# Spacer tiles that shift where the float32r operands of a fused retention and two-layer MoE kernel begin in SBUF

## The chip, the cores and the metric

The kernel runs on one core of a Trainium2 chip. The metric is device time of one execution in microseconds (us); lower is better. Engines: PE is TensorE (PEld its weight loads), DVE VectorE, ACT ScalarE, POOL GpSimd, SP SyncE, which issues most transfers.

## The reference

```python
def _attn_ref(q, k, v):            # (4, 8, 768, 64) each
    gamma = 1.0 - 2.0 ** (-5.0 - np.arange(H))
    for t in range(S):
        state = gamma * state + einsum('bhd,bhe->bhde', k[:, :, t], v[:, :, t])
        y[:, :, t] = scale * einsum('bhd,bhde->bhe', q[:, :, t], state)
...
def _moe_ref(x, w_gate, w_val, w_out, rms_g):     # 3072 tokens, 512 -> 1536 -> 512
    xn = x / sqrt(mean(x * x) + 1e-06) * rms_g
    g = xn @ w_gate
    return silu(g) * (xn @ w_val) @ w_out
...
def _moe2_ref(x, w_in, w_out, g_ln):              # 512 -> 1024 -> 512
    h = x @ w_in
    solu = h * softmax(h)
    return (layernorm(solu) * g_ln) @ w_out
```

The weights arrive as 64-bit floating-point numbers, which the kernel turns into float32 itself.

## The kernel before

The 3,072 tokens go through in six blocks (`n`, 0 to 5) of 512. Of each block the kernel computes the retention (`att_*`, in chunks of 128 tokens), the root-mean-square norm, the gated layer (`bc_block`) and the second layer (`de_block`). Attention of block n+1 is cut into pieces that are called from slots between the matmuls of block n, so that TensorE is never without work; the order on the engines follows the order of the calls and of a scheduler.

The large matmuls run in float32r on operands that were split into a high and a low part (`split`, lines 86 and 87), and each product is three matmuls: `mm3` (lines 561 to 563).

```python
nc.tensor.matmul(ps, lhsT=lh, rhs=rh, start=start, stop=False)
nc.tensor.matmul(ps, lhsT=lh, rhs=rl, start=False, stop=False)
nc.tensor.matmul(ps, lhsT=ll, rhs=rh, start=False, stop=stop)
```

Here `lhsT` is loaded into the array as weights (128 columns of 4 bytes, 512 bytes in each partition) and `rhs` is streamed (512 columns, 2,048 bytes). Four places call it:

- `gv`: gate and value, 12 groups `g` of 128 hidden columns in each block. It loads w4 tiles (in the trace `w`), or CV for odd groups of block 0, and streams xnh and xnl. 24 matmuls a group into the banks GB and VB (the first group of all in halves of 256 columns).
- `cmm`: output of the gated layer. It loads wo tiles or, for odd groups of block 0, CV, and streams r2 tiles (`r`). 12 matmuls a group into X0 to X3.
- `d_mm`: first product of the second layer. It loads x2 tiles (`x`) and streams w2ih and w2il. 24 matmuls for each of 4 token tiles of a block.
- `e_mm`: second product. It loads r2 tiles and streams w2oh and w2ol. 24 matmuls for each token tile (the last of all in halves).

In block 0 the weights are loaded as 64-bit words (`load64`), turned into float32 (`conv`), split, used, and stored to `scr` in HBM; blocks 1 to 5 load the split form from there (`w_load`).

SBUF tiles come from two pools, `cp` (fixed tiles) and `wp` (rings of buffers). They are laid out one behind another in the order in which the program first asks for their tags, each rounded up to 32 bytes, so every tile has a fixed byte address in its partition. Slices that TensorE loads or streams begin at whole multiples of 512 bytes inside their tile, so a tile's address modulo 512 is that of all its slices. Before the change these are:

| tiles | address modulo 512 |
|---|---|
| w2ih (with QK), w2il (with KV), xT, xnh, xnl, U, ssq, w2oh | 128 |
| w2ol, which is also CV; mtab, qtab | 224 |
| ident | 384 |
| the rings: x2, r2, f4, st, w4, wo, rq, rk, rv, kd, qd, kst, qhl, A | 448 |

Of the kernel before, what the change touches and what calls it, by code (L numbers as in the profile page):

```python
# [9 lines left out]
F32 = mybir.dt.float32  # L10
F32R = mybir.dt.float32r
# [7 lines left out]
P = 128  # L19
# [21 lines left out]
def retention_moe_kernel(ctx: ExitStack, tc: tile.TileContext, qk0, q2, kt, kv, wpk, w2i, w2o,  # L41
                         rg, gl, sel, mtab, qtab, ktab, utab, out):
    nc = tc.nc
    cp = ctx.enter_context(tc.tile_pool(name="cp", bufs=1))
# [11 lines left out]
    EB = [GV[0], XB[1], XB[2], XB[3]]  # L56


    QK = cp.tile([P, NCB, 2, 4, P], F32, tag="w2ih", name="QK")
    KV = cp.tile([P, NCB, 2, 512], F32, tag="w2il", name="KV")  # L60
    w2 = {}
# [10 lines left out]
    def wt(tag, shape, dt, bufs):  # L72
        cnt[0] += 1
        return wp.tile(shape, dt, tag=tag, name=f"{tag}_{cnt[0]}", bufs=bufs)
# [10 lines left out]
    def split(hi, lo, src, lo_eng=None):  # L85
        nc.scalar.copy(hi, src)  # L86
        (lo_eng or nc.vector).tensor_tensor(out=lo, in0=src, in1=hi.bitcast(F32), op=ALU.subtract)  # L87
# [119 lines left out]
    def att_yu(gc, u, Y):  # L207
# [4 lines left out]
        if u:  # L212
            sq = f4()[:, 0, :].rearrange("p (a i) -> p a i", a=4)
            nc.scalar.activation(sq, xT[:, :, cs], AF.Square)
            nc.vector.tensor_reduce(out=ssq[:, cs], in_=sq.rearrange("p a i -> p i a"), axis=AX.X, op=ALU.add)

    rinv = cp.tile([P, NCB], F32, tag="rinv", name="rinv")

    def rms_1(bank):
# [86 lines left out]
    def first_load(c):  # L306
        nc.sync.dma_start(QK[:, c], qk0[c])
        nc.sync.dma_start(KV[:, c], kv[c].rearrange("u p x -> p u x"))

    def first_scores(c, banks, halves=(0, 1)):  # L310

        for hh in halves:
            r = slice(64 * hh, 64 * hh + 64)
            for p in range(4):
                nc.tensor.matmul(banks[hh][:, p * P:p * P + P], lhsT=QK[r, c, 1, p, :], rhs=QK[r, c, 0, p, :],
                                 start=True, stop=True)
# [19 lines left out]
    def first_qd(c):  # L336
        qd = wt("r2", [P, 4, P], F32, 8)
        nc.gpsimd.tensor_tensor(out=qd, in0=QK[:, c, 0], in1=qtab_t, op=ALU.mult)
        return qd
# [85 lines left out]
    NG = NB * NM  # L425

    scr = [[dp.tile([P, 2, 512], F32, tag=f"scr{m}_{p}", name=f"scr{m}_{p}") for p in range(3)] for m in range(NM)]
    CV = cp.tile([P, 4, 2, 512], F32R, tag="w2ol", name="CV")

    wide = {}  # L430

    def load64(key):
# [53 lines left out]
    def wtile(part):  # L486
        return wt("w4" if part < 2 else "wo", [P, 2, 512], F32R, 4 if part < 2 else 2)
# [15 lines left out]
    def w_split(g, part):  # L503
# [3 lines left out]
        t = done64.pop((g, part))  # L507
        w = wtile(part) if g % 2 == 0 else CV[:, part if part < 2 else 2 + g // 2 % 2]
        split(w[:, 0, :], w[:, 1, :], t, nc.gpsimd if 0 < g and (part + g) % 2 else nc.vector)
# [251 lines left out]
    def warm(n, bank, rhs):  # L761
        for _ in range(n):
            nc.tensor.matmul(bank[:, 0:P], lhsT=ones, rhs=rhs, start=True, stop=True)

    warm(WARM, GV[1], ones)
    nc.sync.dma_start(QK[:, 0], qk0[0])
    nc.sync.dma_start(mtab_t, mtab)
# [13 lines left out]
    make_identity(nc, ident)  # L781
    mhalf = cp.tile([P, 16], F32, tag="mhalf", name="mhalf")
    nc.gpsimd.memset(mhalf, -0.5)
    nc.gpsimd.memset(U0, 0.0)
    for t in U:
        nc.gpsimd.memset(t, 0.0)
# [178 lines left out]
```

## Time and profile before

| | |
|---|---|
| time, three runs | 1050.81, 1052.34 (median), 1052.58 us |
| profiled execution: span from the first to the last instruction | 1049.7 us |
| PE busy | 1028.7 us, 98% |
| PEld busy | 818.8 us, 78% |
| DVE, ACT, POOL busy | 52%, 39%, 31% |
| DMA | 181.10 MB, mean 173 GB/s |

Of the profiled execution nothing is known beside its span; the runs' median is 2.6 us above it. Matmuls overlap, and their ends are modelled, so a matmul's own duration (about 400 ns for 512 columns) is longer than the distance between the starts of two of them. The rate of TensorE is read from starts in the timeline.

### The profile page before, as it was taken

The numbers are of one execution on the slowest core, as the hardware profiler recorded it, in microseconds if no ns is written. First come the engines' busy times: TensorE is split into PE (matmuls) and PEld (weight loads), VectorE is DVE, ScalarE is ACT, GpSimd is POOL, SyncE is SP. The second block draws the span as 40 slices with busy tenths as digits, with TensorE's granted clock in tenths as the row PEclk, the third lists the DMA queues.
The fourth block names the chain that finished last, engine by engine and source line by source line (L and its number), as shares of the span: only waits on it lengthen the run. The fifth ranks groups of instructions, "written<-read, shape, count | busy, mean of one in ns | idle before, by whom it ended". The sixth has DMA issues, their size and how long they took to land.

```text
span 1049.7 us, 14176 instructions
## 1 busy us (share of the span) xinstructions
PE 1028.7 (98%) x5174; PEld 818.8 (78%) x5174; DVE 542.9 (52%) x1014; ACT 412.2 (39%) x785; POOL 329.4 (31%) x414
## 2 busy tenths in 40 slices
PE   9999999999999999999999999999999999999998
PEld 7877776777878887777777777778777777888887
DVE  5887676886376633344682343482435466111162
ACT  3666655564344432223352232343322325111243
POOL 6886773774134311111250011141211014000031
PEclk9899999999999999999999999999999999999999
DMA  9699996886612015566303566501655510455301
GB/s 345 215 341 382 340 364 260 300 311 211 202 50 71 11 61 190 181 213 206 113 21 118 201 203 221 190 21 30 216 196 200 176 56 21 141 195 185 101 1 41
DMA packets 60485, 181.10 MB, mean 173 GB/s; under 512 B 7168, under 2 KB 7552, under 8 KB 60416
## 3 DMA queue, kind: packets, MB, share of 16 engines
q1 hardware_dynamic: 51632, 155.03, 43.5%
q10 hardware_dynamic: 8784, 25.17, 6.1%
q8 instruction: 41, 0.67, 0.3%
q14 instruction: 28, 0.23, 0.1%
HBM read 153.96 MB, written 26.21 MB: 172 GB/s over the span
## 4 chain that ended last, share of the span: by engine, by line
PE 84%; DVE 7%; DMA 3%; issue 2%; POOL 2%; ACT 1%; SPq 0%; ACTq 0%; POOLq 0%; DVEq 0%
PE X L562 11%; PE X L563 11%; PE X L561 11%; PE GB L561 7%; PE GB L563 7%; PE GB L562 7%; PE VB L561 7%; PE VB L563 7%; PE VB L562 7%; PE YB L158 1%; PE SB L138 1%; DVE st L466 1%; DVE r L87 1%; PE YB L155 1%; DVE st L479 1%
## 5 line engine op out<-in xcount | busy, mean ns | idle before, releaser
L578 DVE TENSOR_TENSOR f<-VB,f 128x512 f32<-128x512 f32 x72 | 49.6, 689 | 171.5 <-PE VB L563 156.1
L128 POOL TENSOR_TENSOR qd<-rq,qtab_t 64x256 f32<-64x256 f32 x68 | 56.5, 831 | 228.8 <-PE YB L155 148.4
L561 PE MATMUL GB<-xnh,w 128*128 128x512 f32 (+1 forms) x268 | 107.3, 400 | 0.2 <-ACT w L86 0.2
L561 PE MATMUL VB<-xnh,w 128*128 128x512 f32 (+1 forms) x268 | 107.1, 400 | 0.0
L562 PE MATMUL GB<-xnl,w 128*128 128x512 f32 (+1 forms) x268 | 106.4, 397 | 0.0
L563 PE MATMUL GB<-xnh,w 128*128 128x512 f32 (+1 forms) x268 | 106.0, 396 | 0.3 <-DVE w L87 0.3
L562 PE MATMUL X<-r,wo 128*128 128x512 f32 x264 | 104.5, 396 | 0.9 <-DVE r L87 0.9
L563 PE MATMUL VB<-xnh,w 128*128 128x512 f32 (+1 forms) x268 | 105.3, 393 | 0.0
L562 PE MATMUL VB<-xnl,w 128*128 128x512 f32 (+1 forms) x268 | 105.2, 393 | 0.0
L563 PE MATMUL X<-r,wo 128*128 128x512 f32 x264 | 103.7, 393 | 0.0
L561 PE MATMUL X<-r,wo 128*128 128x512 f32 x264 | 98.3, 397 | 0.5 <-ACT r L86 0.5
L606 ACT ACTIVATE f<-GB 128x512 f32<-128x512 f32 x72 | 42.8, 595 | 137.4 <-PE GB L563 136.7
L86 ACT CAST r<-f 128x512 fp32r<-128x512 f32 x72 | 44.6, 619 | 115.6 <-DVE f L578 115.2
L467 POOL TENSOR_TENSOR st<-st,x 128x512 int32<-128x512 int32 x52 | 69.9, 1345 | 41.5 <-ACT x L464 12.0
L87 DVE TENSOR_TENSOR r<-f,r 128x512 fp32r<-128x512 f32 x72 | 60.9, 845 | 30.0 <-ACT r L86 29.6
L144 DVE TENSOR_TENSOR A<-SB,s 128x256 f32<-128x256 f32 x64 | 27.0, 422 | 94.3 <-ACT s L142 94.0
L678 POOL TENSOR_TENSOR sm<-sm 128x1 f32<-128x1 f32 x24 | 5.3, 223 | 205.2 <-DVE sm L656 173.4
L142 ACT COPY s<-SB 128x256 f32<-128x256 f32 x64 | 24.0, 374 | 101.7 <-PE SB L138 101.7
L561 PEld LDWEIGHTS GB<-xnh,w 128*128 128x128 f32 x268 | 51.1, 191 | 12.5 <-issue 0.9
L563 PEld LDWEIGHTS GB<-xnh,w 128*128 128x128 f32 x268 | 51.0, 190 | 11.7 <-DVE w L87 0.8
L561 PEld LDWEIGHTS VB<-xnh,w 128*128 128x128 f32 x268 | 50.6, 189 | 12.1 <-issue 1.2
L563 PEld LDWEIGHTS VB<-xnh,w 128*128 128x128 f32 x268 | 50.5, 188 | 12.2 <-POOL w L87 0.4
(241 smaller groups left out, 2359.9 us busy)
## 6 DMA issues: line engine op xcount, KB each, us to landing
w<-scr SPq DMA_DIRECT2D x120, 512.0 KB, 3.3
wo<-scr SPq DMA_DIRECT2D x60, 512.0 KB, 3.3
x<-in_wpk SPq DMA_DIRECT2D x36, 512.0 KB, 6.2
rq<-in_q SPq DMA_DIRECT2D x40, 256.0 KB, 3.3
rv<-in_kv SPq DMA_DIRECT2D x40, 256.0 KB, 3.6
scr<-CV ACTq DMA_DIRECT2D x18, 512.0 KB, 6.3
scr<-w ACTq DMA_DIRECT2D x12, 512.0 KB, 6.4
out<-f ACTq DMA_DIRECT2D x23, 256.0 KB, 2.0
```

Source lines behind the costliest of these rows:

```text
L86: nc.scalar.copy(hi, src)
L87: (lo_eng or nc.vector).tensor_tensor(out=lo, in0=src, in1=hi.bitcast(F32), op=ALU.subtract)
L128: nc.gpsimd.tensor_tensor(out=qd[r], in0=tq4[r, :, hh, :], in1=qtab_t[r, 2 * u:2 * u + 2, :], op=ALU.mult)
L138: nc.tensor.matmul(SB[:, hh * 256:hh * 256 + 256], lhsT=kst[:, hl + hh, :], rhs=qhl[:, hl + hh].rearrange("p s i -> p (s i)"), start=True, ...
L142: nc.scalar.copy(s2, s4[:, :, 1, :])
L144: nc.vector.tensor_tensor(out=A, in0=s4[:, :, 0, :], in1=s2, op=ALU.add)
L467: nc.gpsimd.tensor_tensor(out=ti, in0=ti, in1=lo, op=ALU.add)
L561: nc.tensor.matmul(ps, lhsT=lh, rhs=rh, start=start, stop=False)
L562: nc.tensor.matmul(ps, lhsT=lh, rhs=rl, start=False, stop=False)
L563: nc.tensor.matmul(ps, lhsT=ll, rhs=rh, start=False, stop=stop)
L578: nc.vector.tensor_tensor(out=a, in0=GV[1], in1=silu[:, 0, :], op=ALU.mult)
L606: nc.scalar.activation(s[:, 0, :], GV[0], AF.Silu)
```

## The change

Two spacer tiles, of 320 and 192 bytes in each partition, are allocated and never written or read. The tile CV, with the tag that w2ol takes over, is asked for earlier, before the small tiles rinv and rsum. Nothing else is touched, and the instructions of all five engines stand in the same order as before, with the same waits.

```diff
@@ -56,6 +56,10 @@
     EB = [GV[0], XB[1], XB[2], XB[3]]
 
 
+    def spacer(n, name):
+        cp.tile([P, n // 4], F32, tag=name, name=name)
+
+    spacer(320, "sp0")
     QK = cp.tile([P, NCB, 2, 4, P], F32, tag="w2ih", name="QK")
     KV = cp.tile([P, NCB, 2, 512], F32, tag="w2il", name="KV")
     w2 = {}
@@ -214,6 +218,7 @@
             nc.scalar.activation(sq, xT[:, :, cs], AF.Square)
             nc.vector.tensor_reduce(out=ssq[:, cs], in_=sq.rearrange("p a i -> p i a"), axis=AX.X, op=ALU.add)
 
+    CV = cp.tile([P, 4, 2, 512], F32R, tag="w2ol", name="CV")
     rinv = cp.tile([P, NCB], F32, tag="rinv", name="rinv")
 
     def rms_1(bank):
@@ -425,8 +430,6 @@
     NG = NB * NM
 
     scr = [[dp.tile([P, 2, 512], F32, tag=f"scr{m}_{p}", name=f"scr{m}_{p}") for p in range(3)] for m in range(NM)]
-    CV = cp.tile([P, 4, 2, 512], F32R, tag="w2ol", name="CV")
-
     wide = {}
 
     def load64(key):
@@ -781,6 +784,7 @@
     make_identity(nc, ident)
     mhalf = cp.tile([P, 16], F32, tag="mhalf", name="mhalf")
     nc.gpsimd.memset(mhalf, -0.5)
+    spacer(192, "sp1")
     nc.gpsimd.memset(U0, 0.0)
     for t in U:
         nc.gpsimd.memset(t, 0.0)
```

The addresses modulo 512 after it:

| tiles | before | after |
|---|---|---|
| w2ih (with QK), w2il (with KV), xT, xnh, xnl, U, ssq, w2oh | 128 | 448 |
| w2ol, CV | 224 | 448 |
| the rings (x2, r2, f4, w4, wo, qd, ...) | 448 | 448 |
| mtab, qtab | 224 | 32 |
| ident | 384 | 192 |

The rings lie 512 bytes higher than before, and the tiles of the first row 320 bytes higher.

## Rows read from the trace of the kernel before

**Rows 1.** The page, busy time of the engines, and TensorE's granted clock in 40 slices.
```profile
PE 1028.7 (98%) x5174; PEld 818.8 (78%) x5174; DVE 542.9 (52%) x1014; ACT 412.2 (39%) x785; POOL 329.4 (31%) x414
...
PEclk9899999999999999999999999999999999999999
```

**Rows 2.** The page, the chain that ended last, shares by engine.
```profile
PE 84%; DVE 7%; DMA 3%; issue 2%; POOL 2%; ACT 1%; SPq 0%; ACTq 0%; POOLq 0%; DVEq 0%
```

**Rows 3.** TensorE's waits, whole span: total us, times, longest us.
```profile
PE GB L563 <- DVE r L87: 2.8, 2, 1.8
PE X L562 <- DVE r L87: 2.8, 3, 1.9
```

**Rows 4.** Groups of matmuls by shape: count | busy us, mean ns | idle before.
```profile
L561 PE MATMUL VB<-xnh,w 128*128 128x512 f32 x260 | 104.8, 403 | 0.0
...
L561 PE MATMUL X<-r,wo 128*128 128x512 f32 x264 | 98.3, 397 | 0.5 <-ACT r L86 0.5
...
L669 PE MATMUL X<-ident,f 128*128 128x128 f32 x120 | 17.9, 273 | 1.5 <-POOL f L658 1.5
```

**Rows 5.** Timeline of TensorE, block 5: start us, us, instruction; 24 of `gv`, 12 of `cmm`.
```profile
919.96 0.39 PE L561 MATMUL GB<-xnh,w 128*128 128x512 f32 x1
...
925.56 0.39 PE L561 MATMUL X<-r,wo 128*128 128x512 f32 x1
...
926.25 0.40 PE L561 MATMUL X<-r,wo 128*128 128x512 f32 x1
926.49 0.39 PE L562 MATMUL X<-r,wo 128*128 128x512 f32 x1
926.72 0.39 PE L563 MATMUL X<-r,wo 128*128 128x512 f32 x1
...
928.08 0.39 PE L563 MATMUL X<-r,wo 128*128 128x512 f32 x1
928.30 0.39 PE L561 MATMUL GB<-xnh,w 128*128 128x512 f32 x1
```

**Rows 6.** Timeline of the weight loads beside the first of them.
```profile
920.20 0.19 PEld L563 LDWEIGHTS GB<-xnh,w 128*128 128x128 f32 x1
```

**Rows 7.** Timeline, block 0: `cmm` with CV, 12 intervals.
```profile
64.66 0.40 PE L561 MATMUL X<-r,CV 128*128 128x512 f32 x1
...
67.45 0.39 PE L561 MATMUL GB<-xnh,CV 128*128 128x512 f32 x1
```

**Rows 8.** Timeline, block 0: two `cmm` with wo (11 intervals from 76.14; 9 from 95.54).
```profile
75.81 0.50 PE L561 MATMUL X<-r,wo 128*128 128x512 f32 x1
76.14 0.39 PE L562 MATMUL X<-r,wo 128*128 128x512 f32 x1
...
78.68 0.39 PE L561 MATMUL GB<-xnh,w 128*128 128x512 f32 x1
...
95.54 0.39 PE L561 MATMUL X<-r,wo 128*128 128x512 f32 x1
...
97.58 0.39 PE L561 MATMUL X<-r,wo 128*128 128x512 f32 x1
```

**Rows 9.** Timeline: `e_mm`, 37 intervals, and `d_mm`, 24 intervals.
```profile
324.50 0.40 PE L562 MATMUL X<-w2ol,r 128*128 128x512 f32 x1
...
333.06 0.39 PE L563 MATMUL X<-w2oh,r 128*128 128x512 f32 x1
...
873.63 0.40 PE L561 MATMUL VB<-w2ih,x 128*128 128x512 f32 x1
...
879.23 0.39 PE L561 MATMUL GB<-xnh,w 128*128 128x512 f32 x1
```

**Rows 10.** Busy us of PE, PEld, DVE, ACT, POOL in three stretches, granted clock, DMA share, GB/s.
```profile
35.00:168.00 133.00, 129.85 (x681) 101.78 (x680) 104.07 (x149) 86.26 (x149) 100.11 (x91) 0.97 0.92 339
168.00:350.00 182.00, 176.52 (x868) 140.56 (x867) 117.74 (x209) 86.95 (x169) 77.39 (x85) 1.00 0.53 181
350.00:520.00 170.00, 170.00 (x859) 134.83 (x858) 75.41 (x153) 54.58 (x109) 33.50 (x57) 1.00 0.44 147
```

## The prediction

> **What bounds the kernel now.** I read the totals first: TensorE's matmuls are in flight for 98% of the span, at a granted clock of 9 or more tenths in every slice but one [rows 1], so nearly all of the run is at the higher of its two levels, 2.4 GHz. A busy TensorE isn't proof of a limit, because matmuls overlap, so I went to the chain of work that ended last: 84% of it is TensorE, 7% VectorE, 3% DMA [rows 2]. Then TensorE's own waits: the longest totals are 2.8 us [rows 3]. Nothing that another engine does holds TensorE up for long; what sets the time is how fast TensorE gets from one matmul to the next. Most of these are float32r matmuls of 512 columns. By the loops there are 3,696: 71 full groups in `gv` of 24 (1,704), 72 calls of `cmm` of 12 (864), 24 of `d_mm` of 24 (576), 23 full ones of `e_mm` of 24 (552). The groups of instructions agree: 264 for the first matmul of `cmm` with wo, a third of 792 [rows 4].
>
> The duration in those rows, about 0.40 us, is no price: matmuls overlap. The price is the distance from one start to the next, so I took the timeline. In the last attention-free stretch a block of 24 `gv` matmuls runs from 919.96 to 925.56 us: 5.60/24 = 233.3 ns each. The 12 of `cmm` that follow run to 928.30: 2.74/12 = 228.3 ns, and the six intervals from 926.72 to 928.08 take 1.36/6 = 226.7 [rows 5]. So the same instruction with the same shape has two paces. What differs is where operands lie. While a matmul streams, the weights of the next one are loaded: the load that starts at 920.20 us beside the second matmul is that of the third, and is in flight for 0.19 us [rows 6]. In `cmm` the streamed tile (r2) and the loaded one (wo) both begin at 448 modulo 512; in `gv` the streamed xnh and xnl begin at 128, the loaded w4 at 448.
>
> Two more places bear that out. The `cmm` whose weights lie in CV (224) streams the same r2 tiles in the same order, and takes 2.79/12 = 232.5 ns, with no quick end [rows 7]; so it isn't that `cmm` streams the same two tiles over and over. And an aligned `cmm` in the same busy stage runs at 226.7 ns (2.04/9) from its first matmul [rows 8]. `d_mm` (128 against 448) stands at 5.60/24 = 233.3; `e_mm`, which streams 128 and 224 by turns against 448, at 8.56/37 = 231.4 [rows 9].
>
> **The change part by part.** No instruction is added, removed or moved: the order on all five engines is the same, waits included. The spacers are never written, so they cost no time. Only addresses change, and of these the ones that matter put all float32r tiles at 448, the place that `cmm` with wo has today. DMA writes into the ring buffers keep their place modulo 512.
>
> *The intervals.* 3,696 matmuls stand in 170 unbroken runs in TensorE's order (attention, transposes or sums stand between them). I leave out each run's last interval and its first, which is a start (75.81 to 76.14 is 0.33 us) [rows 8]: 3,696 - 340 = 3,356. Of these 792/3,696 are aligned now, 719. The rest is unaligned: `gv` and `d_mm` 2,280/3,696, 2,070; `e_mm` 501; `cmm` with CV 65. Settled aligned pace: 226.7 ns. So: 2,070 x (233.3 - 226.7) = 13.7 us; 501 x (231.4 - 226.7) = 2.4; 65 x (232.5 - 226.7) = 0.4; and the 719, whose groups are now cut off after 12, 719 x (228.3 - 226.7) = 1.2. Together 17.6 us.
>
> *The price of a start.* An aligned run doesn't always settle at once. After an attention piece one group needed 2.54 us for 11 intervals, 46 ns over 11 x 226.7 [rows 8]; the one behind `gv` needed 1.16 us for its first five, 27 ns over [rows 5]; the one at 95.54 nothing [rows 8]. Bounds 0 and 46 ns a run; I take 20, nearer to the middle case, since some start settled: 170 x 20 ns = 3.4 us. Bounds 0 and 7.8 us. Left: 14.2 us.
>
> *What is late next.* A quicker TensorE asks earlier for what others deliver. From 350 to 520 us VectorE is busy 75 of 170 us and GpSimd 34, and TensorE without a gap: room enough. But in the first block, 35 to 168 us, the DMA engines are busy 92% at 339 GB/s, with VectorE at 104 of 133 us [rows 10]. Its 432 matmuls carry 432/3,696 of the gain, 1.7 us. If the transfers set the pace there, all of it is lost; if not, none; TensorE's waits on converted weights are short but the transfers have little slack, so I take half, 0.8 us. Between 168 and 350 VectorE has 118 of 182 us, and I charge nothing. Left: 13.4 us.
>
> *The other tiles.* `ident` goes from 384 to 192 while the transposed f4 stays at 448; U goes from 128 to 448, where qd is. No row shows either pair at its new place. The two paces of the 512-column form differ by 7 ns; with that either way on the 192 transposes, 120 of which have a row [rows 4], the bound is 1.3 us up or down, and I take zero. The 256-column pieces of `gv` and `e_mm`, 96 matmuls, could give 0.6 us; left out of the sum, kept in the range. Tables that VectorE and GpSimd read (mtab, qtab, utab, ssq) move too: hidden behind TensorE's work, at those engines' idle shares.
>
> Sum: 13.4 us off the profiled execution's 1049.7 us gives a span of 1036.3. The median of the runs is 2.6 us above that span, and I carry this over: 1038.9, say 1039.0 us.
>
> **A rule against it.** The rows show two paces that go with the operands' places [rows 5, 7]. The Trainium skill, page "TensorE: Matmul & The Clock Gate", section "Step-by-step: what each phase is for", says that the array has two independent read ports, and that loading the next tile's weights takes no bandwidth from the running matmul. By that rule the places can't matter and the sum would be 0. The trace doesn't agree: 232.5 and 226.7 ns in one form of instruction with the same streamed tiles.
>
> **The rivals.** *Nothing happens* (1052.3 us): the place of the tiles isn't what parts the two paces, but something that goes with them, such as the engine activity around a `cmm`, or CV being written nearby. For it: `e_mm` at 231.4 lies between, with no aligned pair, so the place modulo 512 alone doesn't make the pace. Against it: the two `cmm` of [rows 7, 8], 31 us apart, the same code, one with CV and one with wo. Chance 0.09. The Trainium skill's rule above (page "TensorE: Matmul & The Clock Gate") gives this case too.
>
> *Slower.* With both at 448, weight load and stream start at the same byte modulo 512, and in long runs of one kind (`gv`: 24) they meet each other again and again, where `cmm`'s runs of 12 end early. The longest intervals among the aligned rows are 0.24 us (926.25 to 926.49) [rows 5]. Locked there, `gv` and `d_mm` lose 6.7 ns, `e_mm` 8.6, `cmm` 11.7: `cmm` with CV 7.5: 13.9 + 4.3 + 8.4 + 0.5 = 27 us, 1079. It decides from a mean above 231.9 ns, which is the weighted mean of today's four paces. Against it: after the sixth matmul the aligned group stays at 226.7. Chance 0.05.
>
> *Most is given back* (1044 to 1048): every run pays 46 ns and the first two blocks, some 30% of the matmuls, keep nothing because DMA and VectorE set their pace. 17.6 - 7.8 = 9.8; less 30%, 6.9; 1045.4. Chance 0.08.
>
> **How the numbers follow.** My forecast has 0.78; its own range is 1034 (no start cost, nothing lost: 1052.3 - 17.6 = 1034.7, and 0.6 for the 256-column pieces) to 1044.3 (46 ns a run and the first block lost: 17.6 - 7.8 - 1.7 = 8.1). To hold eight in ten the range goes on to 1046, into the third rival. About 0.2%, 2.1 us, is what a measurement of this kernel can tell from no change. Faster: 0.78 + 0.08 = 0.86; same 0.09; slower 0.05.
>
> **What would show it.** In the timeline of 900 to 1000 us a `gv` block of 24 should take 5.44 us instead of 5.60, a block of 36 with its `cmm` 8.16 instead of 8.34. `d_mm` should fall from 233.3 to about 227, `cmm` with CV from 232.5, and aligned `cmm` with wo should show its quick end from the first matmul where `gv` stands ahead. If `gv` stays at 233, the places don't matter and I am wrong at the root; if it falls, but the time doesn't, look at the first block's DMA and at what starts cost. The clock should stay as it is, and the order of instructions too. I would also be wrong if the settled pace turned out to hang on the distance in steps larger than 512 bytes, which the spacers leave as they are.

## The result, and the profile after

The changed kernel takes 1041.62 us (median of 4 runs, 1040.31 to 1042.41), the kernel before 1052.46 in the runs taken with it: ratio 0.9901, 95% interval 0.9871 to 0.993. That is 10.8 us of gain; 13.4 were forecast, and 1041.62 lies inside the range of 1034 to 1046. The four runs of the kernel before include one of 1066.30 us; the other three have a median of 1052.34. The profiled execution has a span of 1038.5 us against 1049.7.

The page of the changed kernel, beside [rows 1, 2]:

```profile
PE 1014.7 (98%) x5174; PEld 817.8 (79%) x5174; DVE 542.5 (52%) x1014; ACT 412.5 (40%) x785; POOL 329.5 (32%) x414
...
PEclk9999998999999999999999999999999999999999
...
PE 80%; DVE 8%; issue 4%; POOL 4%; ACT 2%; DMA 1%; SPq 0%; ACTq 0%; POOLq 0%; DVEq 0%
```

Busy shares, clock and counts are nearly as they were, and the reader learns little from them: TensorE is still "98% busy", and it has 80% of the chain where it had 84%. What changed is seen in starts. The timeline of TensorE in block 5, beside [rows 5] (start us, us, instruction; `mm3` is now at lines 564 to 566), and `d_mm`, beside [rows 9]:

```profile
865.86 0.39 PE L564 MATMUL VB<-w2ih,x 128*128 128x512 f32 x1
...
871.30 0.39 PE L564 MATMUL GB<-xnh,w 128*128 128x512 f32 x1
...
919.40 0.39 PE L564 MATMUL GB<-xnh,w 128*128 128x512 f32 x1
...
922.12 0.39 PE L564 MATMUL VB<-xnh,w 128*128 128x512 f32 x1
...
924.84 0.39 PE L564 MATMUL X<-r,wo 128*128 128x512 f32 x1
...
927.56 0.39 PE L564 MATMUL GB<-xnh,w 128*128 128x512 f32 x1
```

24 `gv` matmuls go from 919.40 to 924.84: 5.44 us, 226.7 ns each, where [rows 5] had 5.60. The 12 of `cmm` behind them take 2.72 us, and the 36 together 8.16. `d_mm` has 5.44/24 = 226.7 as well. The matmul's own duration is still 0.39: only the distance between starts shows the change.

Block 0 on the same view, beside [rows 7, 8]: a `cmm` with CV, and the `cmm` with wo that starts after an attention piece.

```profile
64.86 0.39 PE L564 MATMUL X<-r,CV 128*128 128x512 f32 x1
...
67.58 0.39 PE L564 MATMUL GB<-xnh,CV 128*128 128x512 f32 x1
...
76.15 0.39 PE L565 MATMUL X<-r,wo 128*128 128x512 f32 x1
...
78.67 0.39 PE L564 MATMUL GB<-xnh,w 128*128 128x512 f32 x1
```

With CV: 2.72/12 = 226.7, where it was 232.5. With wo: 2.52 us for 11 intervals, 27 ns over the settled pace (before: 46).

**Where the time came from.** The 5,174 matmuls of the two traces pair off one to one, in the same order. I split the distances between successive 512-column matmuls at 300 ns. The short ones, some 3,370, fell from a mean of 232.2 to 228.1 ns: 13.7 us less. The long ones, which hold waits and stretches at half pace, grew by 3.8 us, all of it in the first 195 us (nine distances passed from short to long, and of those only what exceeds the short mean is counted here). Everything else fell by 1.2 us. Sum: 13.7 - 3.8 + 1.2 = 11.1 us. So TensorE's own gain is what was forecast, and the shortfall is in waits.

One place carries most of that. TensorE in block 0 after the change, where `cmm` waits for r2 (in brackets: idle time, and who ended it):

```profile
162.90 1.21 PE L564 MATMUL X<-r,CV 128*128 128x512 f32 x4 [1.94 <-ACT r L90]
...
165.97 0.79 PE L565 MATMUL X<-r,CV 128*128 128x512 f32 x1 [1.85 <-DVE r L91]
166.56 0.63 PE L566 MATMUL X<-r,CV 128*128 128x512 f32 x1
166.98 0.63 PE L565 MATMUL X<-r,CV 128*128 128x512 f32 x1
...
169.12 0.63 PE L566 MATMUL X<-r,CV 128*128 128x512 f32 x1
```

and the same two waits in the kernel before:

```profile
161.73 1.19 PE L561 MATMUL X<-r,CV 128*128 128x512 f32 x4 [0.48 <-ACT r L86]
...
164.82 0.50 PE L562 MATMUL X<-r,CV 128*128 128x512 f32 x1 [1.90 <-DVE r L87]
```

The first wait is 1.5 us longer after the change, although TensorE is quicker: r2 itself came later, by 1.2 us. What held it is shown further down, beside a repeat. After the two waits the starts stand 0.43 us apart instead of 0.23, for some 4.9 us. The windows further down show the granted clock there.

### The profile page after: what moved, and what is told of

It is laid out like the page before. It is cut to its first block, busy times and chain, and to the rows that moved or that the text cites. A ratio compares the mean times of both kernels' runs of the same rounds, so it can differ in the third digit from the quotient of the medians.

```text
span 1038.5 us, 14176 instructions
## 1 busy us (share of the span) xinstructions
PE 1014.7 (98%) x5174; PEld 817.8 (79%) x5174; DVE 542.5 (52%) x1014; ACT 412.5 (40%) x785; POOL 329.5 (32%) x414
## 4 chain that ended last, share of the span: by engine, by line
PE 80%; DVE 8%; issue 4%; POOL 4%; ACT 2%; DMA 1%; SPq 0%; ACTq 0%; POOLq 0%; DVEq 0%
PE X L565 11%; PE X L566 11%; PE X L564 11%; PE GB L564 7%; PE GB L566 7%; PE GB L565 7%; PE VB L564 6%; PE VB L566 6%; PE VB L565 6%; POOL st L470 2%; DVE st L469 1%; PE YB L162 1%; PE SB L142 1%; PE YB L159 1%; DVE st L482 1%
## 5 line engine op out<-in xcount | busy, mean ns | idle before, releaser
L564 PE MATMUL GB<-xnh,w 128*128 128x512 f32 (+1 forms) x268 | 105.5, 394 | 1.2 <-ACT w L90 0.9
L564 PE MATMUL VB<-xnh,w 128*128 128x512 f32 (+1 forms) x268 | 106.0, 396 | 0.0
L566 PE MATMUL GB<-xnh,w 128*128 128x512 f32 (+1 forms) x268 | 104.2, 389 | 0.3 <-DVE w L91 0.3
L566 PE MATMUL VB<-xnh,w 128*128 128x512 f32 (+1 forms) x268 | 104.2, 389 | 0.0
L90 ACT CAST r<-f 128x512 fp32r<-128x512 f32 x72 | 44.6, 619 | 113.3 <-DVE f L581 113.0
L564 PEld LDWEIGHTS GB<-xnh,w 128*128 128x128 f32 x268 | 50.5, 188 | 12.6 <-ACT w L90 1.4
L565 PEld LDWEIGHTS GB<-xnl,w 128*128 128x128 f32 x268 | 50.5, 188 | 11.4 <-DVE xnl L286 1.2
L564 PEld LDWEIGHTS VB<-xnh,w 128*128 128x128 f32 x268 | 50.5, 188 | 11.0 <-issue 1.2
L565 PEld LDWEIGHTS X<-r,wo 128*128 128x128 f32 x264 | 49.6, 188 | 11.9 <-DVE r L91 1.6
```

## The experiments

**Which address counts: all tiles at 128.** Without the first spacer, and with CV moved as in the change:

```diff
-    spacer(320, "sp0")
```

> All float32r tiles begin at 128 modulo 512 instead of 448 (no first spacer, 192 bytes before the rings, CV moved as in the change). Theory 1, the distance between streamed and loaded tile sets the pace, equal is quick: gv, d_mm and cmm settle at 226.7 ns as in the change, 1040 to 1043 us. Theory 2, the place of the streamed tile itself counts and 448 is the quick one: everything streams from 128, gv and d_mm stay at 233.3 ns, cmm rises to 233, 1052 us or more.

1040.78 us (1038.19 to 1044.57) against 1051.25; ratio 0.987 (0.9777 to 0.9964). A block of 24 `gv`:

```profile
912.23 0.39 PE L563 MATMUL GB<-xnh,w 128*128 128x512 f32 x1
...
917.67 0.39 PE L563 MATMUL X<-r,wo 128*128 128x512 f32 x1
```

5.44 us again; the short intervals have a mean of 228.1 ns, as after the change. So it is not the place 448 that is quick, but that both tiles have the same one. One spacer does it.

**How the pace goes with the distance.** Five kernels give the pairs of tiles different distances (streamed minus loaded, modulo 512), by the sizes of three spacers: ahead of xT, ahead of U0 and w2oh, and sp1.

```diff
-    spacer(320, "sp0")
+    spacer(96, "sp2")      # ahead of xT;       e2 96, e3 96,  e4 64,  e9 320, e10 96
+    spacer(96, "sp3")      # ahead of U0, w2oh; e2 96, e3 96,  e4 256, e9 64,  e10 32
-    spacer(192, "sp1")
+    spacer(64, "sp1")      #                    e2 64, e3 128, e4 192, e9 64,  e10 32
```

> Spacers give other distances, streamed minus loaded modulo 512: gv 32, d_mm 448, e_mm 128; cmm with wo stays at 0. Theory 1a, only an equal place is quick: gv, d_mm and e_mm settle at 231 to 234 ns, cmm at 226.7 after its start, about 1052 us. Theory 1b, the pace is slow only in a stretch of distances around 192: gv at 32 and d_mm at 448 come to 226.7, about 1041 us.

> Distances gv 480, d_mm 384, e_mm 64. Theory 1a (only equal places are quick): all three at 231 to 234 ns, about 1052 us. Theory 1b (slow only around 192): all three near 226.7, about 1041 us.

> Distances gv 256, d_mm 192 as in the kernel before, e_mm 0 as in the change. Both theories: d_mm 233.3 ns, e_mm settles at 226.7. Theory 1a: gv 231 to 234. Theory 1b: gv at 256 is either, the edge of the slow stretch. If instead all paces move together with gv, the pace belongs to the whole program and not to the pair of tiles. About 1048 to 1052 us.

> Distances, streamed minus loaded modulo 512: gv 64, d_mm 256, e_mm 128; cmm with wo 0. Theory of a period of 256 bytes: d_mm at 256 settles at 226.7 ns as gv did at 256, gv at 64 and e_mm at 128 stay at 230 to 234. Theory that gv's quick 256 belonged to gv's tiles alone: d_mm at 256 stays at 232 to 234.

> Distances gv 128, d_mm 32, e_mm 160; cmm with wo 0. If only multiples of 256 are quick: gv 231 to 234, d_mm 233.3, e_mm 230 to 234, about 1050 us. If half a period (128) is in any way better than a quarter, gv at 128 is quicker than the 233.1 to 233.5 that it has at 32, 192 and 480, where e_mm at 128 stood at 232.5.

First and last start of a block of 24 in e2 (`gv`, distance 32):

```profile
911.36 0.40 PE L565 MATMUL GB<-xnh,w 128*128 128x512 f32 x1
...
916.96 0.40 PE L565 MATMUL X<-r,wo 128*128 128x512 f32 x1
```

in e4 (`d_mm` at 192, then `gv` at 256), with its clock:

```profile
PEclk6599998999999999999999999999999999999999
...
881.92 0.39 PE L565 MATMUL VB<-w2ih,x 128*128 128x512 f32 x1
...
887.52 0.39 PE L565 MATMUL GB<-xnh,w 128*128 128x512 f32 x1
...
919.36 0.39 PE L565 MATMUL GB<-xnh,w 128*128 128x512 f32 x1
...
924.79 0.39 PE L565 MATMUL X<-r,wo 128*128 128x512 f32 x1
```

in e9 (the last 12 of `d_mm` at 256, then `gv` at 64):

```profile
872.35 0.39 PE L565 MATMUL X<-w2ih,x 128*128 128x512 f32 x1
...
875.07 0.40 PE L565 MATMUL GB<-xnh,w 128*128 128x512 f32 x1
...
915.57 0.40 PE L565 MATMUL GB<-xnh,w 128*128 128x512 f32 x1
...
921.08 0.40 PE L565 MATMUL X<-r,wo 128*128 128x512 f32 x1
```

and in e10 (`gv` at 128):

```profile
920.55 0.40 PE L565 MATMUL GB<-xnh,w 128*128 128x512 f32 x1
...
926.14 0.39 PE L565 MATMUL X<-r,wo 128*128 128x512 f32 x1
```

Worked out in this way (time of the block by its intervals), `gv` and `d_mm` of all these kernels:

| distance modulo 512 | modulo 256 | ns a matmul | where |
|---|---|---|---|
| 0, 256, 256 | 0 | 226.7 | `gv` after; `gv` e4; `d_mm` e9 |
| 32, 32 | 32 | 233.3 | `gv` e2; `d_mm` e10 |
| 64 | 64 | 229.6 | `gv` e9 |
| 128, 384 | 128 | 232.9 | `gv` e10; `d_mm` e3 |
| 192, 192, 448 | 192 | 233.3 | `gv` and `d_mm` before, `d_mm` e4; `d_mm` e2 |
| 480 | 224 | 233.3 | `gv` e3 |

The distance counts modulo 256 bytes, not 512: theory 1a (only an equal place is quick) fails at 256, theory 1b (slow only around 192) at 32, 384, 448 and 480. `e_mm` agrees, by the means of its short intervals: 228.2 ns at 0 (after) and 228.4 (e4), 229.9 at 64 (e3), 232.6 and 232.4 at 128 (e2, e9), 234.0 at 160 (e10). And `cmm` with wo, at 0 in every kernel, ends its 12 at 226.3 to 226.9 ns in all of them; only its first intervals are longer, the more so where the `gv` ahead is slow. In e4 `gv` is quick and `d_mm` slow within one program and 40 us of one another; in e9 it is the other way round. That leaves nothing for the rival that something around the matmuls sets the pace. Half a period gives nothing; 64 gives a little over half of the gain.

These are single runs, and one kernel's runs lie 2 to 6 us apart (after, all at 128), so the means of all short intervals tell more than the times: before 232.2 ns; e10 232.2 (1052.03 us); e2 232.5 (1051.41); e3, whose `e_mm` is at 64, 231.7 (1046.87); e9 230.2 (1045.96). For e9 that makes 1.92 x 3,370 = 6.5 us, of a gain of 7.0 on the kernel before beside it (1052.99). For e3 it makes 1.6 of 4.5 us between the traces; the rest is 1.5 in waits and 1.5 in what is no 512-column interval. e4's 1057.17 is no measure: its clock stood at about half in the first two slices, as in one execution of the kernel before (below), and of it only paces in one execution are compared.

**Matmuls of 256 columns do not follow.** The same `gv` in halves of 256 columns, in the first group of all: 24 intervals before the change (distance 192), 17 after it (distance 0).

```profile
40.92 0.28 PE L562 MATMUL VB<-xnl,w 128*128 128x256 f32 x1
...
43.75 0.28 PE L562 MATMUL VB<-xnl,w 128*128 128x256 f32 x1
```

```profile
41.52 0.28 PE L566 MATMUL GB<-xnh,w 128*128 128x256 f32 x1
...
43.56 0.28 PE L566 MATMUL VB<-xnh,w 128*128 128x256 f32 x1
```

That is 2.83/24 = 117.9 ns at 192 and 2.04/17 = 120.0 at 0. The halves of `e_mm` have a mean of 119.1 before, 119.8 after, and 113.3 at 64 (e3). So what the table says of distances holds for 512 columns.

**Which of two loads counts.** The three matmuls of `mm3` load the high weights twice and the low ones once. Here x2's tiles are 128 bytes longer, so that in `d_mm` the high weights are at 0 and the low ones at 128 (modulo 256) from the streamed tiles; the rest as in the first experiment.

```diff
-        t = wt("x2", [P, 512], I64, 4)
+        t = wt("x2", [P, 528], I64, 4)[:, 0:512]
...
-                th, tl = wt("x2", [P, 2, 512], F32R, 4), wt("x2", [P, 2, 512], F32R, 4)
+                th, tl = (wt("x2", [P, 1056], F32R, 4)[:, 0:1024].rearrange("p (a b) -> p a b", a=2) for _ in range(2))
```

> All at 128 as in e1_all128, but the x2 tiles are 128 bytes longer, so that d_mm's high weights lie at distance 0 modulo 256 and its low ones at 128. Theory 1, what counts is the pair of a stream and the weight load that runs beside it: the interval after the second matmul of mm3 (it streams while the low weights are loaded) is the long one, 230 to 240 ns, the other two near 227. Theory 2, what counts is the matmul's own weights: the interval after the third (low weights in use) is the long one. If all three stand at 232 to 234, one unequal pair in three is enough to unsettle the whole. gv, cmm, e_mm as in e1_all128; about 1042 us.

1044.33 us, with a mean of 228.7 ns. The start of a block of `d_mm`, and of the `gv` behind it:

```profile
869.28 0.39 PE L563 MATMUL VB<-w2ih,x 128*128 128x512 f32 x1
...
874.82 0.39 PE L563 MATMUL GB<-xnh,w 128*128 128x512 f32 x1
```

5.54/24 = 230.8 ns. By the place in `mm3` the settled intervals of this block are 227 behind the first matmul, 233 behind the second (while the low weights are loaded) and 234 behind the third (which uses them). Neither "the load beside the stream" nor "the weights in use" alone gives that; two of three intervals lengthen. Which access meets which stays open.

**Do the stores of the weights set the first block's pace?** 33 of the 36 stores to `scr` are left out, and later blocks load the three that remain; once in the kernel before, once in the changed one.

```diff
-            nc.sync.dma_start(w.bitcast(F32), scr[m][part])
+            nc.sync.dma_start(w.bitcast(F32), scr[0][part])
...
-        nc.scalar.dma_start(scr[g][part], w.bitcast(F32))
+        if g == 0:
+            nc.scalar.dma_start(scr[0][part], w.bitcast(F32))
```

> The kernel before, but 33 of the 36 stores of split weights in the first block are left out, and the later blocks load the three tiles that were stored of the first group again and again (the same bytes in, other numbers in the result). It takes 17 MB out of the first block. Theory A, the DMA engines set the pace of the first block: its last gate group starts some us earlier than in the kernel before (151 us), and the whole is shorter by as much. Theory B, VectorE's and ScalarE's conversion chain sets it: within 1 us of the kernel before.

> The changed kernel with the same stores left out. Theory A: with the DMA engines relieved, the first 190 us keep the gain from the quicker matmuls, 1.5 to 2 us more than with all stores, so this kernel is 12 to 14 us quicker than the run e5_few_stores_before, where the change itself gave 11. Theory B: the first block still gives the gain back, 10 to 11 us between the two.

Without the stores: 1049.16 us, ratio to the kernel before 0.9991 (0.9943 to 1.004). Without them and with the change: 1040.41, ratio 0.9868 (0.9805 to 0.9932). Neither theory forecast either run. The last gate group starts at 156.5 us without the stores and at 151.0 in the kernel before, so later and not earlier, and the 8.7 us between the two are less than both the 12 to 14 of theory A and the 10 to 11 of theory B. The windows of a stretch of the first block (busy us of PE, PEld, DVE, ACT, POOL, granted clock, DMA share, GB/s), in the kernel before:

```profile
60.00:85.00 25.00, 25.00 (x130) 19.18 (x129) 21.58 (x31) 17.46 (x31) 19.55 (x16) 1.00 1.02 390
```

and in it without the stores:

```profile
60.00:85.00 25.00, 24.59 (x128) 18.86 (x127) 20.76 (x30) 18.53 (x32) 19.55 (x16) 1.00 0.68 206
```

The DMA share falls from 1.02 to 0.68, and TensorE issues 128 matmuls instead of 130. VectorE, ScalarE and GpSimd, which convert and split the weights, stay as busy as they were (20.8, 18.5 and 19.6 of 25 us). Leaving stores out also moves some instructions, so these two runs are compared with each other rather than with the rest; their orders are the same, and between them the spacers gained 0.1 us up to 245 us and 8.5 in all. With transfers at two thirds of what they were, the first block still kept nothing. That does not part the transfers from the conversions: the chain of the kernel without stores, from 95 to 175 us, still has 17.8% and 7.5% in loads of 64-bit weights. And the 8.5 us hold two falls of the clock: over 520 to 530 and 695 to 705 us the granted clock is 0.83 with the spacers and 1.00 without, and the lead drops from 4.1 to 2.6 us and from 4.6 to 3.1 there.

**What two executions of one kernel differ by.** The kernel before and the changed one, once more each.

> The kernel before, profiled once more. If the conversion of the weight that ScalarE took up at 147.4 us comes at the same time within 0.5 us, the traces can be compared place by place; if it moves by 1 to 2 us, the loss of 2.2 us there in the changed kernel is a matter of the execution.

> The changed kernel, profiled once more. If the 2.2 us lost between 141 and 148 us come again, they belong to the change; if the loss is away or elsewhere, and the span is 1036 to 1037, it was the execution.

The kernel before took 1069.23 us, again with two slices at about half clock (15.8 us lost by 35 us), so it says nothing on this. The changed one took 1037.22, span 1035.4, and the loss of its first execution is away. ScalarE's conversion of a weight, at 147.42 us in the kernel before, came at 148.61 in the first execution and at 145.70 in the repeat. What it stood behind is in the chain of the kernel before, a load of a weight and the store that ScalarE's queue issues just ahead:

```profile
137.88 9.10 DMA w<-scr
147.05 0.33 ACTq L510
147.42 0.77 ACT x L464
```

The same store and conversion after the change, and in the repeat:

```profile
148.24 0.33 ACTq L513 DMA_DIRECT2D scr<-wo  x1
148.61 0.76 ACT L467 ACTIVATE x<-x,two 128x512 f32<-128x512 uint32 x1 [4.24 <-DVE U L189]
```

```profile
145.33 0.33 ACTq L513 DMA_DIRECT2D scr<-wo  x1
145.70 0.78 ACT L467 ACTIVATE x<-x,two 128x512 f32<-128x512 uint32 x1 [1.96 <-DVE st L469]
```

The load landed at 146.97, 148.16 and 145.25 us (with all at 128 at 146.90), 9.1, 10.8 and 8.7 us (10.0) after its issue, and in all four executions the store went out 0.08 us later. (The brackets name VectorE; the landing is read from the trace's record of the load.) From there to 163 us nearly every instruction of ScalarE, VectorE and GpSimd starts 1.1 to 1.2 us later than in the kernel before, in the repeat 1.7 earlier, and r2 with them. Why the load took longer in one execution stays open.

The two waits of 162.90 and 165.97 us in the repeat:

```profile
160.02 1.20 PE L564 MATMUL X<-r,CV 128*128 128x512 f32 x4 [0.76 <-ACT r L90]
...
163.08 0.50 PE L565 MATMUL X<-r,CV 128*128 128x512 f32 x1 [1.87 <-DVE r L91]
```

Windows around them, in the order the kernel before, the changed one, the changed one again:

```profile
165.00:171.00 6.00, 6.00 (x21) 4.83 (x22) 5.75 (x10) 4.57 (x9) 0.24 (x1) 0.72 0.69 263
```

```profile
165.00:171.00 6.00, 5.04 (x13) 4.07 (x14) 5.62 (x9) 4.13 (x8) 1.38 (x2) 0.51 0.85 295
```

```profile
165.00:171.00 6.00, 5.83 (x25) 4.35 (x24) 4.01 (x8) 3.28 (x7) 0.00 (x0) 1.00 0.43 163
```

The same program gets 13 matmuls through in these 6 us at a granted clock of 0.51 (the lower level, 1.2 GHz), or 25 at 1.00. Ahead of that stand waits of 1.94 and 1.85 us in the one, of 0.76 and 1.87 in the other. But waits alone do not part them: the kernel before had only 0.48 and 1.90 us, and a clock of 0.72 in this window. In the pair with few stores TensorE waited 0.84 and 0.93 us near 525 us in both kernels, and the clock fell in one of them. What decides stays open. Ahead of a matmul that both executions have (181.62 us in the one, 177.21 in the other) the two executions differ by 4.4 us: 1.7 were there ahead of the first wait, 1.2 came with it and 1.5 behind it.

## Why the prediction was right

The lead of each changed kernel over its partner without spacers, at the same matmul (us; the time is the partner's):

| | after over before | the repeat over before | few stores, with over without spacers |
|---|---|---|---|
| 189 | -1.6 | +2.8 | +0.2 |
| 321 to 323 | +0.8 | +4.0 | +1.2 |
| end | +11.1 | +14.2 | +8.5 |

**The intervals** (17.6 us forecast). The mechanism held at every place that was named: `gv` and `d_mm` 233.3 to 226.7, CV 232.5 to 226.7, `cmm` behind `gv` quick from its first matmul. The marks, 5.44 and 8.16 us, came to the hundredth. That the distance counts was shown by the scan, not only by the change, and only for matmuls of 512 columns. One row stays unexplained: `e_mm` before had distances of 192 and 288 by turns, both in the slow class, and yet 231.4 ns [rows 9].

**The price of a start** (3.4 us forecast, 20 ns a run). Mis-sized a little: the short intervals of the changed kernel have a mean of 228.1, 1.4 ns above 226.7; times 3,370 that is 4.7 us, or 28 ns for each of 170 runs. The intervals then gain 13.7 us instead of 14.2. The 256-column pieces, for which 0.6 us was kept in the range, give nothing. These 13.7 are the steady part: the repeat has 13.7 too, the kernel with all at 128 has 13.6, and few stores 13.6.

**What is late next** (0.8 us forecast). This term was mis-sized: the long intervals grew by 3.8 us in the profiled execution and 4.1 with all at 128, and in the repeat they fell by 0.1. (With few stores it was 3.5, of which 2.7 came behind 323 us, with the two falls of the clock.) The first block gave between -1.6 and +2.8 us against the 0.9 that were expected of it. Up to 150 us the lead was +1.2, +1.8 and +1.6 us (change, repeat, all at 128), near the 1.6 that the short intervals gave up to there; what became of it was decided behind that, by the two waits near 160 us and by the clock, in each execution anew. The reason that I named, DMA engines 92% busy [rows 10], holds at this place: one load, landing 8.7 to 10.8 us after its issue, held ScalarE's conversions and with them r2. I priced a share of the block's gain where the trace has one landing; the 9.10 us of it stood in the chain of the kernel before, among the 3% DMA of [rows 2]. The fall of the clock behind a wait, 1.5 us here, had no term at all. Transfers are not the whole of it: with their share at 0.65 over 35 to 168 us the block kept none of the gain either, and the waits of TensorE there are ended by ScalarE and VectorE, which with GpSimd convert and split the weights. That the chain of these three sets the pace of that block is argued; no run shortened it alone.

**The other tiles** (0, within 1.3 us). The transposes did not change; what is neither a 512-column interval nor a wait fell by 1.2 us.

**From the span to the median.** 2.6 us were carried over; the changed kernel's median is 3.1 above its profiled span. Each run's own time is 1.7 or 1.8 us above its own span; the rest is where the profiled execution happens to lie among the runs.

**How near the sum came, and luck.** Between the profiled executions the gain is 11.2 us against 13.4: 0.5 less in the intervals, 3.0 more in waits, 1.2 back from the rest. The repeat would have stood at 14.2. So the intervals were forecast, and how near the total came hangs on the execution.

**The rivals.** *Nothing happens* is out: one program has both paces at once, by distance. The rule named with it is that loading the next weights takes no bandwidth from the running matmul (the Trainium skill, "TensorE: Matmul & The Clock Gate", "Step-by-step: what each phase is for"). The runs do not agree with it for these float32r operands: 6.6 ns a matmul hang on the bytes' places, though which access meets which is not shown. *Slower*, a lock at 0.24, did not appear: the twelve unbroken `gv` blocks behind 200 us stand at 226.7 to 230.6 ns a matmul. *Most is given back* was half right: runs pay 28 ns and not 46, but in the first 245 us the spacers had gained little or nothing (-1.4, +1.7 and +0.1 us in the three pairs). From 323 us on the lead grows by 10.3 and 10.2 us to the end in the two executions of the changed kernel, as the intervals say. With few stores it grows by 7.3, with the two steps back of 1.5 us where the clock falls.

No version beyond the change came out of this that computes the same and is quicker: all at 128, with one spacer, is the same within the spread.

## What to carry to other kernels

Where TensorE is busy without a gap in float32r, with new weights for every matmul of 512 columns, read the distance between starts, not durations or busy shares, for each pair of streamed and loaded tile, and compare it with the tiles' byte addresses modulo 256; if two paces go with that, one spacer may give some 3% of the matmul's pace. Read other shapes by themselves: here 256 columns gained nothing. Cost what is given back stage by stage: a stage in which TensorE waits for others may keep none of it. And compare several executions before a loss of a few microseconds is explained: here one load that landed late, with the fall of the clock behind the wait, moved the total by more than the stage had to win.

## What the runs showed of the hardware that was not expected

- The period is 256 bytes, half of what the change assumed; 64 bytes off costs 2.9 ns a matmul of 512 columns, 32, 128, 192 and 224 cost 6.2 to 6.6. Matmuls of 256 columns are no quicker at 0 (120.0 ns) than at 192 (117.9).
- Two waits of 1.94 and 1.85 us, with four matmuls between them, were followed by 4.9 us of starts 0.43 us apart at a granted clock of 0.51; waits of 0.76 and 1.87 us by none, and shorter ones of 0.48 and 1.90 by a clock of 0.72 over 165 to 171 us.
- A load of 512 KB in the first block, at a DMA share of 1.01 to 1.04, landed 8.7 to 10.8 us after its issue, by execution. A store in ScalarE's queue went out 0.08 us after that landing in four executions of four, and the conversions behind it were late by as much.
- Two executions, one of the kernel before and one with other spacers (e4), began with two slices at a granted clock of 0.5 to 0.6; in the former that cost 15.8 us.
